# Attention and two gated MLPs on one core: another order of the first loads, and transposes without memory columns first

## The chip, the cores and the metric

One core of a Trainium2 chip runs the whole program. The metric is the device time of one execution in microseconds (us), the median over several runs; lower is better. Three runs of the kernel before took 1064.68, 1064.93 and 1065.62 us, so its median is 1064.93 us.

## The reference

The input holds q, k and v for 4 batches, 8 heads, 576 tokens and 64 numbers per head. Cut to what matters:

```python
scores = (q @ k.T) / 8, causal; a = softmax(scores); local = a @ v
q_p = phi(q)                                  # phi(x) = max(x, 0) + exp(min(x, 0))
mem_out = (q_p @ M_prev) / (q_p @ z_prev + 1e-6)
x = sigmoid(beta) * mem_out + (1 - sigmoid(beta)) * local   # 2304 tokens x 512
x = ((sigmoid(x @ w_gate) * (x @ w_val)) @ w_out)           # first MLP, 1536 wide
h = x @ w_in; out = (h * clip(h + 3, 0, 6) / 6) @ w_out2    # second MLP, 2048 wide
```

All of it is in 32-bit floats. The MLP weights come as 64-bit floats and are converted on the core.

## The kernel before, in words

The program has three phases. Phase A (`phase_a`) computes the attention and, as filler between its pieces, the first half of the first MLP; phases B and C do the rest of the MLPs. PE's order is written out by hand (the loop of lines 594 to 639 in a manual schedule). The order of DVE, ACT, POOL and SP is made by a scheduler when the program is built; each of these engines then runs its list strictly in that order.

**Visits and steps.** The attention goes by visits: two heads of one batch (a pair) and one of two ranges of query tokens. `VISITS` lists, for each batch, the four pairs with range 0 (320 tokens) and then the four with range 1 (256 tokens): visits 0 to 3, 4 to 7, 8 to 11 and so on, 32 in all. Each visit takes two steps of the loop. A step issues the scores on PE (L349, tile `s`), the row minima on DVE (L329, tile `m`; the scores are negated, so it is a minimum), and the exponentials on ACT (L367, tile `P`). Scores and the results `m` of the MLP filler share one pool of four PSUM buffers.

**Memory columns.** A row of `P` begins with 64 columns that hold phi(q) times a factor, so that one product with the stacked M_prev and v gives memory and local part together. These columns come from a chain: phi on DVE and ACT (L302 to L304), products with z_prev on POOL (L306, L310, tile `zz`), a sum and reciprocals on DVE (L311, L313, L314, and L392, L394, which also read the softmax sums `l`), and a product on POOL (L382).

**Transposes and pv.** Two or three steps after a visit's exponentials, `transpose_bank` transposes its `P` in blocks of 128x128 on PE (L413), up to four blocks in one PSUM bank, and ACT copies each bank to the tile `T` (L415). Range 0 has 11 blocks in three banks, range 1 has 18 in five. A block is named (row, column block); column block 0 holds the memory columns. One step after the last bank, `pv` (L459) multiplies `T` with the stacked M_prev and v: its first two matmuls read column block 0, the others follow by column block. For visits 0 to 7 it also spreads the factor (L429, tile `rl`) and multiplies (L470).

**Loads.** All DMAs are issued by SP. `load_visit` loads queries and keys (L262, L263, tile `qk`, two buffers), the queries by rows (L265, first part of tile `aux`), for a new batch z_prev (L270, L273, tile `zz`), and v with M_prev (L279, second part of `aux`). `gates` loads beta (L125). `w_load` loads a pair of weight blocks (L147, tile `wst`, two buffers) and `w_convert` converts it: ACT L157, DVE L158, L159, L160, L162, L163, ACT L168, DVE L169.

**The filler.** `moe_a` (L238 to L240) needs converted weights and the attention's output of a whole batch, read back by `moe_x` (tile `xs`, split on ACT L233 and DVE L234).

Of the kernel before, what the change touches and what calls it, by code (L numbers as in the profile page):

```python
# [37 lines left out]
_T = [  # L38
    [(1, 0), (2, 0), (0, 0), (3, 0), (4, 0), (1, 1), (2, 1), (3, 1), (4, 1), (2, 2), (4, 2)],
    [(2 * g + n, j) for g in range(2) for j in range(5) for n in range(2) if j <= n + 3],  # L40
]
BANKS = [[t[n : n + 4] for n in range(0, len(t), 4)] for t in _T]

UNITS = [[(0, 1), (2,)], [(3,), (4,)]]

# [35 lines left out]
class Kernel:  # L81
# [167 lines left out]
        self.visits, self.done = {}, {}  # L249

    def load_visit(self, v):
        if v >= len(VISITS):
            return
        nc = self.nc
        p, ranges = VISITS[v]
        b, h = PAIRS[p]
        qk = self.pa2.tile([128, 2, S], F32, name="qk", tag="qk")
        a = self.pa2.tile([128, 15 * D], F32, name="aux", tag="aux", bufs=3)
        rg = ranges[0]
        (t0, n), nb, j1 = RTOK[rg], len(ROWS[rg]), RANGES[rg][-1] + 1  # L260
        src = self.aux[b, h // 2]
        nc.sync.dma_start(qk[:, 0, t0 : t0 + n], self.qk[b, h // 2, :, 0, t0 : t0 + n])  # L262
        nc.sync.dma_start(qk[:, 1, : t0 + n], self.qk[b, h // 2, :, 1, : t0 + n])  # L263
        q0 = 0 if rg == 0 else 5 * D
        nc.sync.dma_start(a[:, 0 : nb * D], src[:, q0 : q0 + nb * D])  # L265
        if h == 0 and rg == 0:
            z = self.pa2.tile([128, H + H // 2, D], F32, name="zz", tag="zz", bufs=1)
            flat = lambda t: t.rearrange("p h d -> p (h d)")
            one = lambda t: t.rearrange("o h d -> o (h d)")
            nc.sync.dma_start(flat(z[:, 0:H]), one(self.zz[b : b + 1, 0:H]).broadcast_to([128, H * D]))  # L270
            for g in range(2):
                h0 = H + H // 2 * g
                nc.sync.dma_start(  # L273
                    flat(z[64 * g : 64 * g + 64, H:]),
                    one(self.zz[b : b + 1, h0 : h0 + H // 2]).broadcast_to([64, H // 2 * D]),
                )
            self.z = z
        v0 = 5 * D
        nc.sync.dma_start(a[:, v0 : v0 + j1 * 2 * D], src[:, 9 * D : 9 * D + j1 * 2 * D])  # L279
        self.visits[v] = {  # L280
            "pair": PAIRS[p],
            "ranges": ranges,
            "z": self.z,
            "qk": qk,
            "qn": a[:, 0 : nb * D].rearrange("p (r d) -> p r d", d=D),
            "v": a[:, 5 * D :].rearrange("p (j c) -> p j c", j=5),
        }
# [117 lines left out]
    def transpose_bank(self, v, rg, k):  # L405
        nc = self.nc
        pr = self.visits[v]
        if k == 0:
            pr["T", rg] = self.pa2.tile([128, 2304], F32, name="T", tag="T")
        ps = self.ps_t.tile([128, 512], F32, name="t", tag="t")  # L410
        bank = BANKS[rg][k]
        for n, (r, j) in enumerate(bank):
            nc.tensor.transpose(ps[:, 128 * n : 128 * n + 128], self.row(v, rg, r, 128 * j, 128 * j + 128), self.ident)  # L413
        c = 128 * len(bank)
        nc.scalar.copy(pr["T", rg][:, 512 * k : 512 * k + c], ps[:, :c])  # L415

    def spread(self, v, rg):

# [125 lines left out]
    def phase_a(self):  # L544
        nc, tc = self.nc, self.tc
# [10 lines left out]
        stream, c = None, 0  # L556
# [22 lines left out]
        def transposes(t, k):  # L579
            for _ in range(k):  # L580
                if tq and tq[0][0] <= t:
                    a = tq.pop(0)[1]
                    self.transpose_bank(*a)
                    if a[2] == len(BANKS[a[1]]) - 1:
                        vq.append((t + 1, a[:2]))

        t = self.step = 0
        sched = tc.manual_schedule(engines={mybir.EngineType.PE})
        sched.__enter__()
        self.load_visit(0)  # L590
        self.gates()
        self.load_visit(1)
        self.w_load()
        while t < nt or tq or vq:
            self.step = t
            fill = FILL[max(c - 1, 0)]
            first = w = 0
            if t < nt:
                v, rg, i = steps[t]
# [3 lines left out]
                first = w if w <= 512 else 320  # L603
# [19 lines left out]
            if t < nt:  # L623
                self.exponentials(v, i)
                if i == RANGES[rg][-1]:
                    self.normalize(v, rg, 5 <= t < 27)
                    if v < POST:
                        self.memory_rows(v, rg)
                    tq += [(t + (2 if v < 4 else 3), (v, rg, j)) for j in range(len(BANKS[rg]))]
            moe(fill)  # L630
# [3 lines left out]
                self.prep_phi(v + 1)  # L634
            if t >= 7 and t % 2:
                self.w_convert()
            if len(self.wstaged) < 2:
                self.w_load()
            t += 1
        while self.wstaged or self.wkeys:  # L640
# [18 lines left out]
        n = 0  # L659
# [358 lines left out]
```

## Time and profile before

| what | value |
|---|---|
| median of three runs | 1064.93 us |
| the profiled execution's own time | 1065.71 us |
| its span, first to last instruction | 1063.9 us |
| PE busy | 1038.0 us, 98% |
| DVE, ACT, POOL busy | 648.3, 538.6, 84.2 us |
| mean granted TensorE clock | 0.996 |

PE is the engine of the chain that ended last for 89% of the span. The 16,179 instructions are nearly all matmuls and weight loads of PE. The change touches the first 140 us, so the timeline of that stretch is what is to be read, engine by engine.

### The profile page before, as it was taken

What the parts mean: (1) busy time and instruction counts of PE and PEld (TensorE: products, weight loads), DVE (VectorE), ACT (ScalarE), POOL (GpSimd) and SP (SyncE); (2) the same over time, 40 slices, a digit from 0 to 9 for tenths busy, and PEclk for the clock granted to TensorE, in tenths of its full rate; (3) what the DMA queues carried; (4) which work ended last, traced back from release to release, by engine and by line L of the source; (5) the groups of instructions that cost most, each with busy time, mean ns of one, the idle gap of its engine ahead of it and who ended that gap; (6) DMA issues with size and microseconds to landing.
All of it is one profiled execution on the core that took longest, in us unless ns stands there. A gap on an engine that the chain in (4) does not pass through costs nothing.

```text
span 1063.9 us, 16179 instructions
## 1 busy us (share of the span) xinstructions
PE 1038.0 (98%) x5904; PEld 892.6 (84%) x5904; DVE 648.3 (61%) x1549; ACT 538.6 (51%) x1165; POOL 84.2 (8%) x102
## 2 busy tenths in 40 slices
PE   6799999999999999999999999999999999999998
PEld 4467678878887899999888888888888888888886
DVE  6999755454455338888888888743454433643433
ACT  6679885566556644435444344433453433633432
POOL 2213211110111000000000000410002000000000
PEclk9899999999999999999999999999999999999999
DMA  7755642424242215337686877444414542044511
GB/s 220 223 191 184 192 126 75 137 80 124 67 126 80 64 44 180 119 119 254 228 296 246 309 259 276 158 166 177 148 30 158 218 159 99 10 168 169 218 40 59
DMA packets 66239, 164.87 MB, mean 155 GB/s; under 512 B 8432, under 2 KB 41712, under 8 KB 60272
## 3 DMA queue, kind: packets, MB, share of 16 engines
q1 hardware_dynamic: 66160, 163.85, 45.2%
q8 instruction: 46, 0.75, 0.3%
q14 instruction: 33, 0.27, 0.1%
HBM read 122.76 MB, written 41.06 MB: 154 GB/s over the span
## 4 chain that ended last, share of the span: by engine, by line
PE 89%; DVE 4%; DMA 4%; ACT 1%; SPq 1%; issue 1%; POOL 0%; ACTq 0%; DVEq 0%
PE acc L866 18%; PE pa L831 9%; PE pb L831 7%; PE m L238 6%; PE g L240 6%; PE g L238 6%; PE g L239 6%; PE m L239 5%; PE m L240 5%; PE pv L459 5%; PE t L413 4%; PE s L349 4%; PE acc L238 3%; PE acc L240 3%; PE acc L239 3%; DMA xd<-xpr 1%
## 5 line engine op out<-in xcount | busy, mean ns | idle before, releaser
L866 PE MATMUL acc<-wslot,hs 128*128 128x512 f32 x864 | 227.8, 395 | 2.2 <-ACT hs L233 2.2
L866 PEld LDWEIGHTS acc<-wslot,hs 128*128 128x128 f32 x864 | 159.5, 188 | 27.7 <-ACT hs L233 3.5
L831 PE MATMUL pa<-xq,wslot 128*128 128x384 f32 x576 | 117.3, 338 | 1.1 <-ACT u L931 0.6
L831 PEld LDWEIGHTS pa<-xq,wslot 128*128 128x128 f32 x576 | 103.7, 187 | 9.9 <-ACT u L931 0.9
L240 PE MATMUL g<-xs,wslot 128*128 128x468 f32 (+1 forms) x288 | 106.4, 370 | 0.0
L239 PE MATMUL g<-xs,wslot 128*128 128x468 f32 (+1 forms) x288 | 106.3, 369 | 0.0
L238 PE MATMUL g<-xs,wslot 128*128 128x468 f32 (+1 forms) x288 | 104.1, 369 | 0.0
L367 ACT ACTIVATE P<-P,m 128x192 f32<-128x192 f32 (+4 forms) x144 | 83.9, 585 | 28.4 <-DVE m L329 27.3
L238 PE MATMUL m<-xs,wslot 128*128 128x312 f32 x288 | 94.4, 328 | 0.4 <-ACT xs L233 0.4
L239 PE MATMUL m<-xs,wslot 128*128 128x312 f32 x288 | 88.5, 307 | 0.1
L240 PE MATMUL m<-xs,wslot 128*128 128x312 f32 x288 | 88.1, 306 | 0.0
L831 PE MATMUL pb<-xq,wslot 128*128 128x384 f32 x432 | 87.8, 338 | 0.0
L831 PEld LDWEIGHTS pb<-xq,wslot 128*128 128x128 f32 x432 | 77.9, 188 | 6.3
L349 PE MATMUL s<-qk 64*128 64x320 f32 (+3 forms) x320 | 72.5, 491 | 10.3 <-DMA qk<-in_qk 7.1
L895 DVE TENSOR_TENSOR c<-pb,u 128x384 f32<-128x384 f32 x48 | 26.6, 555 | 86.7 <-ACT u L931 85.7
L843 ACT ACTIVATE r<-c,three 128x384 f32<-128x384 f32 x72 | 44.2, 614 | 63.4 <-DVE c L895 63.4
L413 PEld LDWEIGHTS t<-ident,P 128*128 128x128 f32 x464 | 53.6, 144 | 23.2 <-issue 11.9
L234 DVE TENSOR_TENSOR hs<-r,hs 128x384 fp32r<-128x384 f32 x96 | 56.5, 593 | 26.9 <-ACT hs L233 25.4
L413 PE MATMUL t<-ident,P 128*128 128x128 f32 x464 | 67.7, 284 | 3.6 <-POOL P L382 3.5
L329 DVE CUSTOM_DVE_ANT_0 P<-s,mask 128x320 f32<-128x320 f32 (+3 forms) x144 | 62.8, 451 | 13.3 <-PE s L349 13.2
L415 ACT COPY T<-t 128x512 f32<-128x512 f32 (+2 forms) x128 | 65.9, 540 | 8.4 <-PE t L413 8.3
L157 ACT ACTIVATE wf<-wst 128x512 f32<-128x512 f32 (+1 forms) x59 | 43.9, 744 | 43.4 <-DVE wst L163 36.7
(106 smaller groups left out, 1937.9 us busy)
## 6 DMA issues: line engine op xcount, KB each, us to landing
wst<-in_wm SPq DMA_DIRECT2D x68, 512.0 KB, 5.9
wslot<-wd SPq DMA_DIRECT2D x30, 1024.0 KB, 5.1
wd<-wslot SPq DMA_DIRECT2D x16, 1024.0 KB, 4.6
wslot<-wd SPq DMA_DIRECT2D x15, 768.0 KB, 6.4
wd<-wslot SPq DMA_DIRECT2D x8, 768.0 KB, 5.8
qk<-in_qk SPq DMA_DIRECT2D x32, 160.0 KB, 2.4
aux<-in_aux SPq DMA_DIRECT2D x16, 320.0 KB, 3.8
qk<-in_qk SPq DMA_DIRECT2D x16, 288.0 KB, 3.1
```

What stands on the lines that cost most here:

```text
L234: elo.tensor_tensor(lo, src, hi.bitcast(F32), op=ALU.subtract)
L238: nc.tensor.matmul(out, w[0], x[0], start=first, stop=False)
L239: nc.tensor.matmul(out, w[0], x[1], start=False, stop=False)
L240: nc.tensor.matmul(out, w[1], x[0], start=False, stop=last)
L329: self.nc.vector.tensor_tensor_reduce(out=self.row(v, rg, r, 64 + a, 64 + e), in0=ps, in1=mask, scale=-0.125, scalar=3.0e38 if a == 0 else ...
L349: nc.tensor.matmul(ps[:, : e - a], qk[rows, 0, q0 : q0 + 128], qk[rows, 1, a:e], start=True, stop=True)
L367: self.nc.scalar.activation(x, x, AF.Exp, bias=vs["m", rg][:, r : r + 1], scale=-1.0, accum_out=vs["l", rg][:, r : r + 1])
L413: nc.tensor.transpose(ps[:, 128 * n : 128 * n + 128], self.row(v, rg, r, 128 * j, 128 * j + 128), self.ident)
L415: nc.scalar.copy(pr["T", rg][:, 512 * k : 512 * k + c], ps[:, :c])
L459: nc.tensor.matmul(ps[rows, o : o + w], pr["v"][:, j, rows], T[:, c : c + w], start=(n == 0), stop=(n == last), skip_group_check=True,)
L831: nc.tensor.matmul(ps[:, :HC], w[:, i, b, cc], x[:, l, k], start=first and k == 0 and n == 0, stop=last and k == 1 and n == 2, skip_group_ ...
L866: nc.tensor.matmul(a, h[:, i, cc], w[:, l, f], start=first and f == 0 and n == 0, stop=last and f == 1 and n == 2)
```

## The change

Two things are changed.

1. `load_visit` becomes a generator, `load_parts`, which stops once after the queries and keys and the queries by rows. The program now issues these three loads for visits 0 and 1 first, then beta, then the rest (z_prev, v with M_prev) of both. The first `w_load` is no longer ahead of the loop; it comes at the end of step 2.
2. `BANKS` holds, for each bank, its place in the list of blocks. Range 0's banks are now blocks 7 to 10, 4 to 6 and 0 to 3 of the same list, in this order; range 1's are 4 to 7, 12 to 15, 16 and 17, 0 to 3, and 8 to 11. The first bank of range 0 holds no memory columns, the second one block of them and the third three. Each bank is copied to the same columns of `T` as its blocks had.

```diff
--- before.py
+++ after.py
@@ -39,7 +39,8 @@
     [(1, 0), (2, 0), (0, 0), (3, 0), (4, 0), (1, 1), (2, 1), (3, 1), (4, 1), (2, 2), (4, 2)],
     [(2 * g + n, j) for g in range(2) for j in range(5) for n in range(2) if j <= n + 3],
 ]
-BANKS = [[t[n : n + 4] for n in range(0, len(t), 4)] for t in _T]
+_B = [[(7, 11), (4, 7), (0, 4)], [(4, 8), (12, 16), (16, 18), (0, 4), (8, 12)]]
+BANKS = [[(a, t[a:e]) for a, e in b] for t, b in zip(_T, _B)]
 
 UNITS = [[(0, 1), (2,)], [(3,), (4,)]]
 
@@ -249,6 +250,10 @@
         self.visits, self.done = {}, {}
 
     def load_visit(self, v):
+        for _ in self.load_parts(v):
+            pass
+
+    def load_parts(self, v):
         if v >= len(VISITS):
             return
         nc = self.nc
@@ -263,6 +268,7 @@
         nc.sync.dma_start(qk[:, 1, : t0 + n], self.qk[b, h // 2, :, 1, : t0 + n])
         q0 = 0 if rg == 0 else 5 * D
         nc.sync.dma_start(a[:, 0 : nb * D], src[:, q0 : q0 + nb * D])
+        yield
         if h == 0 and rg == 0:
             z = self.pa2.tile([128, H + H // 2, D], F32, name="zz", tag="zz", bufs=1)
             flat = lambda t: t.rearrange("p h d -> p (h d)")
@@ -408,11 +414,11 @@
         if k == 0:
             pr["T", rg] = self.pa2.tile([128, 2304], F32, name="T", tag="T")
         ps = self.ps_t.tile([128, 512], F32, name="t", tag="t")
-        bank = BANKS[rg][k]
+        first, bank = BANKS[rg][k]
         for n, (r, j) in enumerate(bank):
             nc.tensor.transpose(ps[:, 128 * n : 128 * n + 128], self.row(v, rg, r, 128 * j, 128 * j + 128), self.ident)
         c = 128 * len(bank)
-        nc.scalar.copy(pr["T", rg][:, 512 * k : 512 * k + c], ps[:, :c])
+        nc.scalar.copy(pr["T", rg][:, 128 * first : 128 * first + c], ps[:, :c])
 
     def spread(self, v, rg):
 
@@ -587,10 +593,10 @@
         t = self.step = 0
         sched = tc.manual_schedule(engines={mybir.EngineType.PE})
         sched.__enter__()
-        self.load_visit(0)
+        loads = [self.load_parts(v) for v in range(2)]
+        next(loads[0]), next(loads[1])
         self.gates()
-        self.load_visit(1)
-        self.w_load()
+        next(loads[0], None), next(loads[1], None)
         while t < nt or tq or vq:
             self.step = t
             fill = FILL[max(c - 1, 0)]
@@ -634,7 +640,7 @@
                 self.prep_phi(v + 1)
             if t >= 7 and t % 2:
                 self.w_convert()
-            if len(self.wstaged) < 2:
+            if t >= 2 and len(self.wstaged) < 2:
                 self.w_load()
             t += 1
         while self.wstaged or self.wkeys:
```

**SP, the first loads** (qk: queries and keys; aux 128x320: queries by rows; aux 128x384: v with M_prev; wst: weights). Before, from the fourth DMA on:

```order
L270 DMA zz<-in_zz 128x512
L273 DMA zz<-in_zz 64x256 x2
L279 DMA aux<-in_aux 128x384
L125 DMA bt_sb<-in_bt 128x20
L262 DMA qk<-in_qk 128x320
L263 DMA qk<-in_qk 128x320
L265 DMA aux<-in_aux 128x320
L279 DMA aux<-in_aux 128x384
L147 DMA wst<-in_wm 128x1024 x2
```

Now, from the fourth DMA on:

```order
L267 DMA qk<-in_qk 128x320
L268 DMA qk<-in_qk 128x320
L270 DMA aux<-in_aux 128x320
L126 DMA bt_sb<-in_bt 128x20
L276 DMA zz<-in_zz 128x512
L279 DMA zz<-in_zz 64x256 x2
L285 DMA aux<-in_aux 128x384 x2
L270 DMA aux<-in_aux 128x320
L267 DMA qk<-in_qk 128x320
L268 DMA qk<-in_qk 128x320
L285 DMA aux<-in_aux 128x384
L148 DMA wst<-in_wm 128x1024 x4
```

The queries and keys of visit 1 moved ahead of zz; the weights moved behind the four loads of visit 2, and both pairs now stand together.

**ACT, the copies of visit 0's transposes** (T<-t) and the first step of the first weight conversion (wf<-wst). Before:

```order
L157 ACTIVATE wf<-wst 128x1024
L367 ACTIVATE P,l<-P,m 128x320
L415 COPY T<-t 128x512
L303 ACTIVATE phw<-phw 128x320
L415 COPY T<-t 128x512
L415 COPY T<-t 128x384
L168 CAST wslot<-wst 128x1024
```

Now:

```order
L373 ACTIVATE P,l<-P,m 128x320 x2
L421 COPY T<-t 128x512
L309 ACTIVATE phw<-phw 128x320
L421 COPY T<-t 128x384
L158 ACTIVATE wf<-wst 128x1024
L421 COPY T<-t 128x512
L373 ACTIVATE P,l<-P,m 128x192 x2
```

The weight step stood ahead of all three copies and now stands between the second and the third.

**DVE, step 11 of the loop** (P,m<-s: a row minimum; wf, wst, wslot: weight conversion). Before:

```order
L329 ISA P,m<-s,mask 128x320
L329 ISA m 128x1
L329 ISA P,m<-s,mask 128x320
L329 ISA m 128x1
L160 SCALAR_TENSOR_TENSOR wst<-wst,wf 128x1024
L311 TENSOR_REDUCE nr<-phw 128x4
L329 ISA P,m<-s,mask,m 128x256
L329 ISA m 128x1
L162 TENSOR_SCALAR wf<-wst 128x1024
L329 ISA P,m<-s,mask,m 128x256
```

Now, from the minimum of the same 320 columns on:

```order
L335 ISA P,m<-s,mask 128x320
L335 ISA m 128x1
L163 TENSOR_SCALAR wf<-wst 128x1024
L320 RECIPROCAL nr<-nr 128x4
L335 ISA P,m<-s,mask 128x320
L335 ISA m 128x1
L164 ISA wst<-wst,wf 128x1024x2
L170 TENSOR_TENSOR wslot<-wst,wslot 128x1024
L159 TENSOR_SCALAR wf<-wf 128x1024
L160 TENSOR_SCALAR wf<-wf 128x1024
L335 ISA P,m<-s,mask,m 128x256
L335 ISA m 128x1
```

Ahead of the first minimum of 256 columns five conversion steps more are done now: those of lines 163, 164, 170, 159 and 160, which are L162, L163, L169, L158 and L159 before the change. The step of line 161 (L160 before) now stands ahead of the first row shown.

## Rows read from the trace of the kernel before

**Rows 1.** Busy time by stretch (stretch, its length, each engine, granted clock, DMA share, GB/s).

```profile
0.00:19.70 19.70, 12.00 (x68) 7.41 (x69) 10.54 (x44) 10.40 (x30) 6.96 (x17) 1.00 0.79 248
19.70:64.00 44.30, 37.04 (x224) 23.82 (x226) 40.35 (x124) 33.26 (x81) 8.55 (x11) 0.92 0.62 187
...
140.00:1063.90 923.90, 916.07 (x5094) 807.02 (x5092) 531.06 (x1192) 430.28 (x892) 50.53 (x55) 1.00 0.43 148
```

**Rows 2.** Timeline, 0 to 22 us, PE (start, length, engine, line, tiles, [idle before <-releaser]).

```profile
9.40 1.14 PE L349 MATMUL s<-qk 64*128 64x192 f32 x4 [2.95 <-DMA qk<-in_qk]
...
12.54 2.55 PE L413 MATMUL t<-ident,P 128*128 128x128 f32 x11 [0.24 <-POOL P L382]
...
15.58 0.69 PE L349 MATMUL s<-qk 64*128 64x192 f32 x4 [0.48 <-DMA qk<-in_qk]
...
16.80 1.81 PE L459 MATMUL pv<-T,aux 128*64 128x320 f32 x9 [0.28 <-ACT T L415]
...
19.53 1.36 PE L349 MATMUL s<-qk 64*128 64x320 f32 x4
```

**Rows 3.** The same timeline: what waited for the first loads.

```profile
4.84 0.33 DVE L302 TENSOR_SCALAR phw<-aux 128x320 f32<-128x320 f32 x1 [3.98 <-DMA aux<-in_aux]
...
7.72 0.22 ACT L128 ACTIVATE a<-bt_sb 128x20 f32<-128x20 f32 x1 [0.33 <-DMA bt_sb<-in_bt]
...
10.47 0.33 DVE L302 TENSOR_SCALAR phw<-aux 128x320 f32<-128x320 f32 x1 [1.32 <-DMA aux<-in_aux]
...
14.62 1.12 ACT L157 ACTIVATE wf<-wst 128x1024 f32<-128x1024 f32 x1 [0.91 <-DMA wst<-in_wm]
...
15.90 0.33 DVE L302 TENSOR_SCALAR phw<-aux 128x320 f32<-128x320 f32 x1 [1.22 <-DMA aux<-in_aux]
```

**Rows 4.** The same timeline: POOL, the first product with zz, the first memory columns.

```profile
6.34 0.72 POOL L310 TENSOR_TENSOR phw<-ph,zz 128x256 f32<-128x256 f32 x1 [3.74 <-DVE ph L304]
...
11.43 1.06 POOL L382 TENSOR_TENSOR P<-ph,nr 128x320 f32<-128x320 f32 x1 [4.08 <-DVE nr L394]
```

**Rows 5.** The same timeline: ACT, last two copies of the first transposes.

```profile
17.02 0.96 ACT L415 COPY T<-t 128x512 f32<-128x512 f32 x2
```

**Rows 6.** Timeline, 20 to 75 us, PE: transposes that waited, pv that did not.

```profile
29.50 1.42 PE L413 MATMUL t<-ident,P 128*128 128x128 f32 x11 [2.35 <-POOL P L382]
...
40.72 1.51 PE L459 MATMUL pv<-T,aux 128*64 128x320 f32 x12
...
42.71 1.68 PE L349 MATMUL s<-qk 64*128 64x320 f32 x6
```

**Rows 7.** Timeline, 20 to 75 us, DVE: the steps of weight conversions.

```profile
55.47 0.69 DVE L158 TENSOR_SCALAR wf<-wf 128x1024 f32<-128x1024 f32 x1 [1.03 <-ACT wf L157]
...
57.19 0.68 DVE L159 TENSOR_SCALAR wf<-wf 128x1024 int32<-128x1024 int32 x1
...
60.54 0.69 DVE L162 TENSOR_SCALAR wf<-wst 128x1024 int32<-128x1024 uint32 x1
...
62.02 1.23 DVE L163 CUSTOM_DVE_ANT_0 wst<-wst,wf 128x2048 uint16<-128x2048 uint16 x1
...
64.77 1.22 DVE L169 TENSOR_TENSOR wslot<-wst,wslot 128x1024 fp32r<-128x1024 f32 x1
```

**Rows 8.** Timeline, 20 to 75 us, PE: a wait for xs, and scores of 448 columns.

```profile
53.97 0.41 PE L238 MATMUL m<-xs,wslot 128*128 128x312 f32 x1 [0.39 <-ACT xs L233]
...
60.08 1.61 PE L349 MATMUL s<-qk 64*128 64x448 f32 x4
```

**Rows 9.** Timeline, 84 to 140 us, PE: pv of visits 9 and 11, the latter in two rows.

```profile
109.06 1.41 PE L459 MATMUL pv<-T,aux 128*64 128x320 f32 x12
...
127.24 1.18 PE L459 MATMUL pv<-T,aux 128*64 128x320 f32 x6
...
130.03 0.86 PE L459 MATMUL pv<-T,aux 128*64 128x256 f32 x6 [1.61 <-ACT T L415]
```

**Rows 10.** Busy time by stretch, PE alone (PE busy, granted clock, DMA share, GB/s).

```profile
45.80:52.50 6.70, 5.77 (x20) 0.50 0.67 218
```

## The prediction

> **What bounds the kernel now.** I read the busy time by stretch first. From 140 us on PE is busy for 916.07 of 923.90 us [rows 1]: whatever the first 140 us lose or win on PE stays in the total, since PE's list is fixed and nothing behind it has slack to give. Between 0 and 19.7 us PE is busy for 12.00 us and DVE for 10.54, so both wait there, and the DMA share is 0.79: the first loads decide. Between 19.7 and 64 us DVE is busy for 40.35 of 44.30 us [rows 1]. That is the view that matters most: there DVE is close to full, every wait of PE hangs on its row minima or on ACT, and both run their lists strictly in order.
>
> Then I read the timelines engine by engine and followed the changed lists through them by hand: an instruction starts when its engine is free and what it reads is there, with the lengths of the rows. A sum of parts that are moved can't do this, since a part moved early on SP comes out late on ACT.
>
> **Start, the gain.** PE's first real wait is 2.95 us for the keys of visit 1 at 9.40 [rows 2]. In the new list of SP the transfers of zz, v and beta no longer stand ahead of them. These came in between 4.84 us, when the first aux ended DVE's wait, and 7.72 us, when beta ended ACT's [rows 3]: 2.9 us. The keys should land at about 6.4, PE needs them then, and the wait goes: -2.95.
>
> **Start, what takes it back.** zz now lands later, by the three loads of visit 1 (7.72 to 10.47: 2.75 us [rows 3]) and by beta (under 0.5, the rest of that stretch). POOL's first product with zz, which started at 6.34 [rows 4], starts at 9.3 to 10. The first memory columns came 5.1 us after it, at 11.43 [rows 4]; 1.32 us of that was DVE's wait for the second aux [rows 3], which falls away. So they start at 9.7 + 3.8 = 13.5 instead of 11.43, and end near 14.3 (12.8 if the chain is tighter, 14.9 if not). The transposes of visit 0 took 2.55 us for 11 [rows 2], 0.23 each. Four now run ahead of the memory columns, seven behind: they end near 15.5, against 15.09 before. The scores of visit 2 then start at about 15.5; before, at 15.58 after 0.48 us of waiting for their keys [rows 2]. Net of the start: **-0.1** (-1.5 to +0.9). Doing the blocks without memory columns first is thus what saves this place from a loss, and no more.
>
> **pv of visit 0.** On ACT the third copy of `T` now stands behind the first step of the weight conversion, and the first two matmuls of pv read exactly that copy. Before, the weights ended ACT's wait at 14.5 (the 0.91 us before 14.62), and the four loads of visit 2 came behind them, the third at 15.9 [rows 3], the fourth some 0.5 later. Now these four come first: weights at 14.5 + 1.9 = 16.4, ACT free of their step 1.0 us later, the copy (0.96 for two [rows 5]) done at 17.9. pv before started at 16.80 and the next scores at 19.53 [rows 2], its middle slowed by the same copies. Without a wait, pv and the spreading take 40.72 to 42.71 [rows 6], 2.0 us, so the next scores start at 19.9 to 20.5: **+0.8** (+0.4 to +1.5).
>
> **Transposes of visit 2.** They waited 2.35 us for POOL's columns [rows 6]. Four of eleven now go ahead, at 0.13 each: 0.5 us are certain; more only if the columns come sooner, but they hang on DVE, whose weight steps have begun. **-0.5** (-2.35 to 0). Elsewhere before 36 us I see nothing that lasts.
>
> **The first filler.** A wait of 0.39 us for the last xs [rows 8] is on ACT's cast; in the new list a weight step (1.0 us to the next start) stands ahead of that cast. **+1.0** (0 to +2).
>
> **Row minima of step 11.** This is the largest term. Ahead of the first minimum of 256 columns DVE now does five more conversion steps. Their lengths are 0.69, 1.23, 1.22, 0.69 and 0.68 us [rows 7], 4.5 together, 4.1 less the 0.08 by which each overlaps its follower. The scores of 448 columns at 60.08 [rows 8] need the PSUM buffers which these minima free, and PE stands still meanwhile. Not all is lost: DVE itself waited 1.03 us for a weight step before [rows 7], a hole that a conversion done sooner may fill. **+3.1** (+1 to +4.1). The conversions are not extra work, but what DVE saves by having done them finds PE already the bound.
>
> **pv of visits 8 to 11.** Where copies come late, pv before did six passes, 1.18 us, ahead of its 1.61 us of waiting [rows 9]; now the copy it waits for is the one that its first matmul reads, so those 1.18 us move behind the wait. At 109.06 there was no wait [rows 9]. Four such visits, at 0 to 1.2 each: **+2.4** as the middle (0 to +4.8).
>
> **Sum.** -0.1 + 0.8 - 0.5 + 1.0 + 3.1 + 2.4 = +6.7 us. The profiled execution took 1065.71 us, so 1072.4; it stands 0.8 above the median of 1064.93, so the median should be **1071.6 us**. All other moved DMAs (SP's list differs in places up to 120 us) I cost at nothing: PE shows no wait for a DMA behind 20 us other than through xs, which is priced. If that cover went, 0.5 to 1 us each.
>
> **The clock.** PE ran at a granted 0.50 (1.2 GHz) from 45.8 to 52.5 us, 5.77 us of busy time [rows 10], after a stretch with gaps; at full speed that work would take 2.9 us less. The row at 15.58 shows four score matmuls in 0.69 us where those at 9.40 took 1.14 [rows 2], so the first 13 to 15 us are slow too, though the granted clock reads 1.00. I leave both as they are in the sum. The Trainium skill (TensorE: Matmul & The Clock Gate, section on HAM oscillation) says that a wait of PE between bursts can return it to half clock, each time anew; by it the longer gap ahead of pv of visit 0 could bring a second slow stretch. The trace neither shows nor excludes this: the gap of 2.35 us at 29.50 brought none.
>
> **The rivals.**
> - *Faster: the start's gain lasts.* If zz is not what the memory columns wait for, or the weights land as early as before, PE keeps the 2.95 us, wins 0.48 and up to 2.35 at visit 2, and meets the minima no later than before: -4, 1061. For it: DVE and ACT are not full before 19.7 us [rows 1]. Against: both lists are in order, and zz and weights are behind more bytes on one queue. It decides itself by whether the first filler matmul, at 50.9 us before, comes sooner. Chance 0.10.
> - *No change.* Start and pv cancel, the five steps fall into DVE's holes (3.95 us between 19.7 and 64 [rows 1]), and the copies are in time: 0 to +2, 1065 to 1067. Chance 0.15.
> - *Slower by a second slow stretch of the clock:* another 2.9 us on top, 1074.5. Chance 0.08. The opposite, the present slow stretch gone, gives 1068.7 and is held in the forecast's range.
> - *Slower, as summed:* 1067 to 1077 by the bounds. Chance 0.67.
>
> **How the numbers follow.** A measurement of this kernel can tell about 0.2%, 2.1 us, from no change. Slower by more: 0.67 + 0.08 = 0.75; within: 0.15; faster by more: 0.10. The range leaves out most of the faster case and the far end of the bounds: 1063.5 to 1076.
>
> **What would show it.** Right: PE's wait at 9.40 gone; POOL's first product with zz near 9.7; ACT's first weight step near 16.4, and pv behind a wait on ACT of 2 us or more that ends near 18; scores of 448 columns that wait about 3 us for DVE near 60; and waits on ACT at the *start* of pv between 100 and 135 us. The first filler matmul should come within 1 us of 50.9. Wrong: if the scores of 448 columns do not wait for the minima, the largest term fails and the result is 1068.5 or less; if pv starts at 17 us, the weights were not late; if the time is below 1063, the start's gain survived the lists.

## The result, and the profile after

The changed kernel takes **1072.23 us** (median of 5 runs, 1069.61 to 1073.38) against 1065.62 us for the kernel before, run beside it: ratio 1.0059, 95% interval 1.0042 to 1.0076. That is slower by 6.6 us. The profiled execution took 1071.09 us, its span is 1069.3 us against 1063.9. Lines of the changed kernel stand 1 to 6 higher: L355 are the scores (L349 before), L335 their row minima, L419 the transposes, L421 the copies to `T`, L465 pv, L158 to L170 the weight conversion.

Busy time by stretch, kernel after (columns as in [rows 1]):

```profile
0.00:19.70 19.70, 11.96 (x49) 6.75 (x51) 10.73 (x50) 11.10 (x35) 6.39 (x18) 1.00 0.78 248
19.70:64.00 44.30, 37.05 (x223) 24.48 (x219) 43.05 (x118) 31.94 (x75) 9.29 (x9) 0.85 0.61 188
...
140.00:1069.30 929.30, 921.73 (x5128) 810.56 (x5124) 532.76 (x1203) 434.03 (x901) 52.04 (x56) 1.00 0.43 148
```

From 140 us on PE again works nearly without a hole. In the middle stretch DVE is fuller than before (43.05 us against 40.35), and the granted clock is 0.85 instead of 0.92.

Timeline, 0 to 22 us, PE, kernel after:

```profile
8.58 1.44 PE L355 MATMUL s<-qk 64*128 64x320 f32 x4
9.94 1.11 PE L419 MATMUL t<-ident,P 128*128 128x128 f32 x4
12.18 1.75 PE L419 MATMUL t<-ident,P 128*128 128x128 f32 x7 [1.12 <-POOL P L388]
13.87 1.01 PE L355 MATMUL s<-qk 64*128 64x192 f32 x4
...
18.30 2.62 PE L465 MATMUL pv<-T,aux 128*64 128x320 f32 x12 [3.01 <-ACT T L421]
```

The wait for the keys of visit 1 [rows 2] is gone, and the scores of visit 2 start at 13.87 instead of 15.58. Then pv of visit 0 stands for 3.01 us in front of its last copy, and all twelve passes follow behind it. POOL and ACT tell why. The same timeline, POOL, then ACT:

```profile
8.59 0.73 POOL L316 TENSOR_TENSOR phw<-ph,zz 128x256 f32<-128x256 f32 x1 [5.99 <-DMA zz<-in_zz]
...
11.41 0.72 POOL L388 TENSOR_TENSOR P<-ph,nr 128x320 f32<-128x320 f32 x1 [1.82 <-DVE nr L400]
```

```profile
14.03 0.56 ACT L421 COPY T<-t 128x512 f32<-128x512 f32 x1
...
15.02 0.46 ACT L421 COPY T<-t 128x384 f32<-128x384 f32 x1
16.65 1.12 ACT L158 ACTIVATE wf<-wst 128x1024 f32<-128x1024 f32 x1 [1.17 <-DMA wst<-in_wm]
17.67 0.58 ACT L421 COPY T<-t 128x512 f32<-128x512 f32 x1
```

POOL's first product with `zz` started later (8.59, released by `zz`, against 6.34 [rows 4]), but the memory columns came at 11.41 as before: the chain behind it took 2.8 us instead of 5.1. The copy that pv waits for stands behind the weight step, as forecast.

Timeline, 20 to 75 us, PE, kernel after: the next scores behind pv of visit 0 (21.91; 19.53 before [rows 2]), then the waits that answer to [rows 6] and [rows 8].

```profile
21.91 0.82 PE L355 MATMUL s<-qk 64*128 64x320 f32 x4
...
30.61 0.98 PE L419 MATMUL t<-ident,P 128*128 128x128 f32 x7 [1.91 <-POOL P L388]
...
36.00 0.81 PE L355 MATMUL s<-qk 64*128 64x320 f32 x4
...
46.08 2.71 PE L355 MATMUL s<-qk 64*128 64x256 f32 x6 [1.79 <-DVE m L335]
...
50.34 0.61 PE L239 MATMUL m<-xs,wslot 128*128 128x312 f32 x1
...
54.25 0.41 PE L239 MATMUL m<-xs,wslot 128*128 128x312 f32 x1 [1.08 <-ACT xs L234]
...
55.44 0.82 PE L355 MATMUL s<-qk 64*128 64x320 f32 x4
...
61.31 1.02 PE L355 MATMUL s<-qk 64*128 64x448 f32 x2
63.18 1.02 PE L355 MATMUL s<-qk 64*128 64x448 f32 x2 [0.86 <-DVE m L335]
```

At 36.00 PE is where it was before (36.09 then), at 55.44 it is 0.5 us behind (54.98 then). The scores of 448 columns wait 0.86 us, not 3.

Timeline, 84 to 140 us, PE: the last scores ahead of pv of visit 8, pv of visits 8 to 11, and the filler behind it. First the kernel before, what [rows 9] doesn't show:

```profile
99.88 0.81 PE L349 MATMUL s<-qk 64*128 64x320 f32 x4
100.62 2.01 PE L459 MATMUL pv<-T,aux 128*64 128x320 f32 x12
...
117.11 1.98 PE L459 MATMUL pv<-T,aux 128*64 128x320 f32 x12
...
130.83 0.41 PE L238 MATMUL m<-ha,wslot 128*128 128x312 f32 x1
```

Kernel after:

```profile
101.35 0.81 PE L355 MATMUL s<-qk 64*128 64x320 f32 x4
103.23 1.41 PE L465 MATMUL pv<-T,aux 128*64 128x320 f32 x12 [1.07 <-ACT T L421]
...
112.87 1.41 PE L465 MATMUL pv<-T,aux 128*64 128x320 f32 x12 [1.70 <-ACT T L421]
...
122.18 1.41 PE L465 MATMUL pv<-T,aux 128*64 128x320 f32 x12 [1.22 <-ACT T L421]
...
133.28 1.41 PE L465 MATMUL pv<-T,aux 128*64 128x320 f32 x12 [2.19 <-ACT T L421]
134.61 0.63 PE L239 MATMUL m<-ha,wslot 128*128 128x312 f32 x1
```

Every one now waits ahead of its first matmul, 6.2 us in all. Before there was one listed wait of 1.61 us, in the middle of pv of visit 11, and the rows of visits 8 and 10 were longer (2.01 and 1.98 us against 1.41), so pv stood a little there too. From the scores of the first row to the filler of the last PE took 30.95 us before and 33.26 after: 2.3 us more. ACT's list shows what the last copy stands behind. The same timeline, ACT, at visit 9:

```profile
109.28 0.47 ACT L421 COPY T<-t 128x384 f32<-128x384 f32 x1
109.64 1.94 ACT L407 ACTIVATE P<-P,l 128x64 f32<-128x64 f32 x5
...
112.25 0.56 ACT L421 COPY T<-t 128x512 f32<-128x512 f32 x1
```

The third copy comes 3 us behind the second, after five normalizing steps of the next visit (1.94 us) and two exponentials. In the kernel before that block also stood there, at 109.22, but behind the last copy (108.15) in this visit; where it stood ahead of it, six passes of pv were already done.

**Where the 5.4 us of span are.** I read how far PE is behind the kernel before at the same matmuls. A good mark is the scores of 320 columns right ahead of pv of visit 8: they start at 99.88 before and at 101.35 after. So the first 100 us lost 1.5 us, and what follows lost 3.9 (span less the mark, called the rest: 964.0 before, 968.0 after): 2.3 us up to the filler behind pv of visit 11, and 1.6 behind that, where PE falls to half clock (last section). The experiments below are read with the same two numbers.

### The profile page after: what moved, and what is told of

Its sections match the earlier page's. It is cut to its first block, busy times and chain, and to the rows that moved or that the text cites. A ratio compares the mean times of both kernels' runs of the same rounds, so it can differ in the third digit from the quotient of the medians.

```text
span 1069.3 us, 16177 instructions
## 1 busy us (share of the span) xinstructions
PE 1040.4 (97%) x5904; PEld 894.6 (84%) x5904; DVE 647.7 (61%) x1549; ACT 539.5 (50%) x1165; POOL 83.2 (8%) x102
## 4 chain that ended last, share of the span: by engine, by line
PE 86%; DVE 8%; ACT 3%; DMA 1%; issue 1%; SPq 0%; DVEq 0%; ACTq 0%
PE acc L872 18%; PE pa L837 9%; PE pb L837 7%; PE g L241 6%; PE m L239 6%; PE g L239 6%; PE g L240 6%; PE m L240 5%; PE m L241 5%; PE pv L465 4%; PE t L419 4%; PE s L355 3%; PE acc L239 3%; PE acc L241 3%; PE acc L240 3%; DVE P L335 1%
## 5 line engine op out<-in xcount | busy, mean ns | idle before, releaser
L355 PE MATMUL s<-qk 64*128 64x320 f32 (+3 forms) x320 | 71.3, 505 | 6.6 <-DMA qk<-in_qk 3.6
L419 PEld LDWEIGHTS t<-ident,P 128*128 128x128 f32 x464 | 54.3, 146 | 24.7 <-issue 14.3
L335 DVE CUSTOM_DVE_ANT_0 P<-s,mask 128x320 f32<-128x320 f32 (+3 forms) x144 | 62.6, 452 | 19.0 <-PE s L355 18.9
L419 PE MATMUL t<-ident,P 128*128 128x128 f32 x464 | 69.8, 287 | 3.6 <-POOL P L388 3.5
L421 ACT COPY T<-t 128x512 f32<-128x512 f32 (+2 forms) x128 | 66.2, 538 | 13.2 <-PE t L419 13.2
L465 PE MATMUL pv<-T,aux 128*64 128x256 f32 (+2 forms) x512 | 59.6, 377 | 9.8 <-ACT T L421 9.7
```

The lines of the kernel that those rows point to most:

```text
L335: self.nc.vector.tensor_tensor_reduce(out=self.row(v, rg, r, 64 + a, 64 + e), in0=ps, in1=mask, scale=-0.125, scalar=3.0e38 if a == 0 else ...
L355: nc.tensor.matmul(ps[:, : e - a], qk[rows, 0, q0 : q0 + 128], qk[rows, 1, a:e], start=True, stop=True)
L421: nc.scalar.copy(pr["T", rg][:, 128 * first : 128 * first + c], ps[:, :c])
L465: nc.tensor.matmul(ps[rows, o : o + w], pr["v"][:, j, rows], T[:, c : c + w], start=(n == 0), stop=(n == last), skip_group_check=True,)
```

## Experiments

**Theory A:** pv's first matmuls need the bank that is copied last; the loss of the banks is PE standing in front of that copy. **Rival B:** the loads are the loss (zz and weights late), as most of my sum had it. **Rival C:** the stretches at half clock come and go by themselves. The summary follows, with "mark" and "rest" from the profiled execution of each kernel. That is one execution, up to 2.9 us from the median of its kernel (first weights early: 1073.48 us against 1076.34), so a difference of 1 or 2 us in them is weak. Line numbers shift between the kernels; the tiles name the instruction.

| kernel | median us | ratio to before (95%) | mark | rest |
|---|---|---|---|---|
| before | 1065.5 | | 99.88 | 964.0 |
| changed | 1072.23 | 1.0059 (1.0042 to 1.0076) | 101.35 | 968.0 |
| banks only | 1074.57 | 1.0088 (1.0075 to 1.0101) | 107.44 | 967.3 |
| loads only | 1062.07 | 0.9972 (0.9961 to 0.9983) | 96.85 | 963.6 |
| changed, old banks from visit 8 | 1066.75 | 1.0013 (1.0005 to 1.0022) | 102.35 | 964.0 |
| changed, old banks in visits 0 to 3 | 1069.92 | 1.0037 (1.0024 to 1.0050) | 98.13 | 970.0 |
| changed, first weights early | 1076.34 | 1.0102 (1.0087 to 1.0117) | 105.92 | 965.8 |
| changed, pv multiplies memory columns last | 1073.60 | 1.0074 (1.0058 to 1.0090) | 106.48 | 965.7 |
| loads only, the same order of pv | 1072.16 | 1.0061 (1.0046 to 1.0075) | 101.65 | 967.7 |
| before, first weights late | 1072.45 | 1.0067 (1.0049 to 1.0085) | 103.58 | 965.8 |
| before, keys of visit 1 early | 1070.97 | 1.0059 (1.0042 to 1.0076) | 102.43 | 965.9 |
| before, conversion cut | 1068.98 | 1.0032 (1.0020 to 1.0044) | 106.10 | 961.1 |
| keys early, conversion cut | 1064.08 | 0.9984 (0.9976 to 0.9993) | 101.97 | 961.6 |
| changed, conversion cut | 1069.51 | 1.0030 (1.0020 to 1.0041) | 101.96 | 965.7 |

**Banks only.** The loads of before, the new banks:

```diff
+        self.load_visit(0)
+        self.gates()
+        self.load_visit(1)
+        self.w_load()
...
-            if t >= 2 and len(self.wstaged) < 2:
+            if len(self.wstaged) < 2:
```

> The changed banks of transposes alone, with the loads in the order of before. Theory A (pv's first matmuls wait for the bank that is copied last, in visits 8 to 11): in the changed kernel these waits, with what the clock loses behind them, carry the lag from 1.5 us at 101 to 6 us at 150, so most of that should stay here: 1068.5 to 1071.5, with four waits of 1 us or more on ACT at the start of pv between 100 and 140 us. Rival B (the loads: zz and weights land late, and the delay is handed down): the banks alone cost nothing, 1064 to 1066.5. Rival C (stretches at half clock that come and go): the time follows the number of such stretches and not the waits.

Measured 1074.57 us: the banks alone lose 9.1 us, more than the whole change. Rival B's 1064 to 1066.5 falls. PE's waits between 100 and 140 us, this kernel (waiting, what for: us in total, times, longest):

```profile
PE pv L465 <- ACT T L421: 5.5, 4, 2.2
```

Four waits, as theory A wants, though one is 0.41 us only; but only 3.3 us of the loss stand behind the mark, and 7.6 ahead of it, which A had not put there (this execution took 1076.44 us, 1.9 above the median).

**Loads only.** The changed kernel with the banks of before:

```diff
-_B = [[(7, 11), (4, 7), (0, 4)], [(4, 8), (12, 16), (16, 18), (0, 4), (8, 12)]]
+_B = [[(0, 4), (4, 8), (8, 11)], [(0, 4), (4, 8), (8, 12), (12, 16), (16, 18)]]
```

> The new order of loads alone, with the banks of before. Theory A: only the lag of the first 100 us is left, 1.5 us, and the transposes behind the memory columns cost up to 1 us more at the start: 1066 to 1069, with no wait at the start of pv between 100 and 140 us. Rival B: nearly all the loss is here, 1070.5 to 1073. Rival C: as the number of stretches at half clock says.

Measured 1062.07 us: **faster than both kernels**, by 3.4 us against before and 10.2 against the changed one. My range for it began at 1066. Timeline, 0 to 22 us, PE, this kernel:

```profile
11.82 2.61 PE L419 MATMUL t<-ident,P 128*128 128x128 f32 x11 [1.86 <-POOL P L388]
14.36 1.01 PE L355 MATMUL s<-qk 64*128 64x192 f32 x4
...
15.59 1.18 PE L465 MATMUL pv<-T,aux 128*64 128x320 f32 x6
17.52 0.65 PE L465 MATMUL pv<-T,aux 128*64 128x256 f32 x4 [0.74 <-ACT T L421]
...
18.87 0.81 PE L355 MATMUL s<-qk 64*128 64x320 f32 x4
```

The transposes now wait 1.86 us for the memory columns, which is what the new banks were to avoid, and the scores of visit 2 come 0.5 us later than in the changed kernel (13.87). But pv of visit 0 does half its passes ahead of the last copy, and the next scores start at 18.87, against 21.91 in the changed kernel and 19.53 before [rows 2]. The first filler matmul comes at 47.49, 3.4 us sooner than before (50.93).

**Old banks from visit 8 on.**

`BANKS_O` is built like `BANKS`, from the old `_B`:

```diff
-        first, bank = BANKS[rg][k]
+        first, bank = (BANKS if v < 8 else BANKS_O)[rg][k]
```

> The changed kernel, but visits from 8 on use the banks of before. Theory A: the waits at the start of pv between 100 and 140 us go, and with them about 4 us: 1067 to 1069. The granted clock between 130 and 140 us should read 1.00 again, since PE doesn't stand still ahead of it. Rival B: no change against the changed kernel, 1071 to 1073. Rival C: 1071 to 1073 also, with the clock still low between 130 and 140 us.

Measured 1066.75 us, 5.5 less than the changed kernel, slightly better than A had it. The rest behind the mark is that of before, 964.0. PE's waits between 100 and 140 us:

```profile
PE pv L466 <- ACT T L422: 2.2, 2, 1.2
```

Both are of the kind that the kernel before shows, inside pv with two or six passes done, and no stretch at half clock is left between 100 and 160 us. Of the 4.0 us that the rest wins, 1.8 come by the filler behind pv of visit 11 (31.43 us from the mark, against 33.26 in the changed kernel); the others come behind it, where the changed kernel has that stretch.

**First weights early.** The changed kernel, `w_load` ahead of the loop again and the condition on `t` taken out:

```diff
         next(loads[0], None), next(loads[1], None)
+        self.w_load()
...
-            if t >= 2 and len(self.wstaged) < 2:
+            if len(self.wstaged) < 2:
```

> The changed kernel, but the first weights are loaded ahead of the loop again, behind the loads of visits 0 and 1. Theory A: pv of visit 0 no longer waits 3 us for its last copy, and PE is 1 to 2.4 us earlier near 22 us; the waits of visits 8 to 11 stay, so 1069.5 to 1072. Rival B: the late weights are the loss, 1065 to 1067.5. Rival C: as the number of stretches at half clock says.

Measured 1076.34 us, worse than A and B had it, and 4.1 us above the changed kernel. PE waits 2.63 us for the keys of visit 2 at 16.25, now behind the weights; pv of visit 0 still waits, and the next scores come at 22.32. So in the changed kernel the late weights are no loss but a gain.

**pv with the memory columns last.** The banks and copies stay; in visits 0 to 3 and 8 to 11 pv begins with block columns 1 and 2. Block column 0 is split, since its 64 columns that nothing else writes need a start of their own:

```diff
+            for g in range(2):
+                o, f = 64 * g, 256 * (1 - g)
+                ops[g] = [
+                    (1, o, 640 + 256 * g, 256, True, False),
+                    (2, o + 128, 1152 + 128 * g, 128, False, False),
+                    (0, o, 320 * g + o, 256, False, True),
+                    (0, f, 320 * g + f, 64, True, True),
+                ]
```

> The changed kernel, but pv of visits 0 to 3 and 8 to 11 multiplies the memory columns last: it begins with what the banks copied first hold, and four of its matmuls can run ahead of the copy of the last bank. Transposes, copies and loads stay as in the changed kernel. Theory A (the loss is pv standing in front of the last bank): the loss of the banks, 10 us over the loads alone at 1062.1, goes for the most part: 1062 to 1066. Rival D (the new order of transposes and copies itself is dearer, whichever part pv reads first): 1070 to 1073, as the changed kernel.

Measured 1073.60 us: a miss for A as a whole, and half a hit. The rest falls from 968.0 to 965.7, the waits at pv from 6.2 to 3.8 us between 100 and 145. But the mark is 5.1 us later than in the changed kernel. Timeline, 0 to 45 us, PE, this kernel:

```profile
15.49 1.55 PE L475 MATMUL pv<-T,aux 128*64 128x256 f32 x8 [0.24 <-ACT T L421]
18.01 1.33 PE L475 MATMUL pv<-T,aux 128*64 128x256 f32 x8 [0.97 <-ACT T L421]
...
20.34 1.44 PE L355 MATMUL s<-qk 64*128 64x320 f32 x4
...
31.39 1.75 PE L419 MATMUL t<-ident,P 128*128 128x128 f32 x7 [3.25 <-POOL P L388]
33.07 1.87 PE L355 MATMUL s<-qk 64*128 64x448 f32 x4
```

pv of visit 0 gains as wanted, the next scores start 1.6 us sooner (20.34 against 21.91). Then the transposes of visit 2 wait 3.25 us for POOL instead of 1.91, and the scores behind them run in 1.87 us for four instead of 1.22, at a granted clock of 0.50 between 32 and 36 us.

**The same order of pv with the old banks and the new loads.** The diff of the run above, with the old `_B` as in the loads only. pv's second matmul now reads the bank that is copied last:

```diff
-_B = [[(7, 11), (4, 7), (0, 4)], ...
+_B = [[(0, 4), (4, 8), (8, 11)], ...
+                ops[g] = [
+                    (1, o, 640 + 256 * g, 256, True, False),
...
```

> The loads alone (1062.1), with the banks of before, but with the order of pv of the run above in visits 0 to 3 and 8 to 11: its second matmul now reads the bank that is copied last. Theory A: pv waits again although transposes and copies stand as in the faster kernel, and loses 4 to 10 us: 1066 to 1072, with waits on ACT at the start of pv between 95 and 135 us. Rival D: 1061 to 1064.

Measured 1072.16 us against 1062.07: 10 us lost by the order of pv alone, with banks and loads those of the fastest kernel. PE's waits between 100 and 140 us:

```profile
PE pv L475 <- ACT T L421: 3.7, 3, 2.2
```

4.8 us of the loss are ahead of the mark and 4.1 behind it, 1.6 of these by the filler behind pv of visit 11 (33.19 us from the mark against 31.61). So which part pv reads first does cost time with transposes and copies as they were, and rival D falls as the whole of the loss. But theory A isn't shown as the whole either: with this order of pv the new banks take 1073.60 us and the old ones 1072.16, so it gave back nothing of what the new banks cost. Ahead of the mark the two changes even add up (96.85 with neither, 101.35 with the banks, 101.65 with the order of pv, 106.48 with both), which A doesn't explain.

**The halves of the loads.** First only the weights late, then only the keys early:

```diff
         self.load_visit(1)
-        self.w_load()
...
-            if len(self.wstaged) < 2:
+            if t >= 2 and len(self.wstaged) < 2:
```

> The kernel before, with the first weights late (from the end of step 2) as the one change. With the new banks, late weights were worth 4.1 us (1072.2 against 1076.3). Theory E (they are the gain of the loads, since visit 2's loads no longer queue behind 2 x 512 KB of weights, and DVE's and ACT's first conversion steps stand later): 1061 to 1063.5. Rival F (the early keys of visit 1 are the gain): 1065 to 1066.5. My prediction's step (late weights cost 0.8 at pv of visit 0 and more at the first filler): 1066 to 1070.

> The kernel before, with only the first half of the change in the loads: queries and keys of visit 1 early, zz later, the weights ahead of the loop as before, the banks as before. Theory E: no gain, 1065 to 1067.5, as the wait for the keys comes back at visit 2, whose loads then stand behind the weights. Rival F: 1061 to 1063.5.

Measured 1072.45 and 1070.97 us: **each half alone loses (7 and 5.5 us), both together gain 3.4.** Theories E and F both fall, and so does my prediction's step (1066 to 1070 for the weights late); a reading that adds one part's gain to the other's can't hold here. Timeline, 20 to 75 us, PE, weights late only:

```profile
40.83 1.22 PE L349 MATMUL s<-qk 64*128 64x256 f32 x2 [3.15 <-DVE xpr L470]
...
57.78 0.63 PE L238 MATMUL m<-xs,wslot 128*128 128x312 f32 x1 [3.68 <-ACT xs L233]
```

Scores wait for a PSUM buffer that DVE's product L470 frees, and the filler for an `xs`, each a wait that the kernel before has at 1.0 and 0.39 us at most. With the keys early only, the waits are 2.58 us for POOL at 29.32 and 1.45 us for DVE at 41.25. One pattern is common to these two, the banks only and the changed kernel with its weights early: the fourth weight conversion starts on ACT between 43.6 and 49.2 us. In the kernel before, the changed one and the loads only it starts between 52.1 and 54.3. That is no cause shown: the two kernels with the other order of pv are as slow and have it at 53.2 and 57.0. PE also ran at half clock for longer, some 17 us with the weights late and 10 with the keys early, against 7 in the kernel before (added up from the granted clock by half microseconds).

**Old banks in visits 0 to 3.** The counterpart of the run with old banks from visit 8 on:

```diff
-        first, bank = BANKS[rg][k]
+        first, bank = (BANKS if v >= 4 else BANKS_O)[rg][k]
```

> The changed kernel, but visits 0 to 3 use the banks of before, the others the new ones (the counterpart of the run with the old banks from visit 8 on). If the two places of the banks' loss are separate, this one gives back the other part: 10.2 us is the whole (1072.2 against 1062.1 for the loads alone), 5.5 of it was from visit 8 on, so 4.7 comes back here: 1066.5 to 1068.5, with the waits on ACT at the start of pv between 100 and 140 us still there. If the early part is only handed down to the later one, more comes back: 1063 to 1065.5. If the early part is not the banks: 1070 to 1073.

Measured 1069.92 us: 2.3 us come back, half of what I had. At the mark it is 3.2 us (98.13 against 101.35), but the waits behind it grow to 6.9 us. The two places of the loss are real, and they aren't quite separate.

**Conversion cut.** Five of DVE's six steps of a conversion and one of ACT's two are left out in the first part:

```diff
-        for hif in self.value(st):
+        hif = st[:, :, :, 1].bitcast(F32)
+        for hif in self.value(st) if self.wide == 1 else [hif]:
             nc.scalar.copy(sl[:, 0], hif)
```

> The kernel before without five of DVE's six steps and the first of ACT's two steps of each weight conversion in the first part of the program (the weights there then are not the right ones); loads, casts and all work of PE stay. DVE loses about 30 us of its busy time before 140 us. Theory G (between 20 and 66 us PE waits for lists of DVE and ACT in which conversion steps stand ahead of what it needs): 1055 to 1062. Otherwise 1064 to 1066. It is the base for the next two.

> The early keys alone (1071.0, 5.5 us above the kernel before), without the same conversion steps. Theory G: the loss is the place of conversion steps in DVE's and ACT's lists, so it goes: within 2 us of the kernel before without these steps. Rival H (the late zz and the loads of visit 2 behind the weights cost it by themselves): 3.5 to 6 us above that kernel.

> The changed kernel without the same conversion steps. Theory A with G: pv's waits for its last bank stay in part, as the copies stand in ACT's list behind exponentials too: 2 to 6 us above the kernel before without these steps. If the conversions were all of the loss of 6.6 us: within 1 us of it.

Measured 1068.98, 1064.08 and 1069.51 us. The first is the surprise: 38.6 us less work on DVE ahead of 140 us, and the kernel is **3.4 us slower**. Theory G, as I had put it, falls. DMA issues between 30 and 62 us (tensor, queue, number, KB each, median us from issue to landing), the kernel with the conversion cut, then the kernel before:

```profile
wst<-in_wm SPq DMA_DIRECT2D x9, 512.0 KB, 5.7
```

```profile
wst<-in_wm SPq DMA_DIRECT2D x4, 512.0 KB, 4.4
```

Timeline, 36 to 64 us, the kernel with the conversion cut, DVE, then PE:

```profile
41.96 0.29 DVE L303 TENSOR_SCALAR phw<-aux 128x256 f32<-128x256 f32 x1 [2.12 <-DMA aux<-in_aux]
```

```profile
44.10 2.66 PE L350 MATMUL s<-qk 64*128 64x448 f32 x4 [3.04 <-DVE m L330]
```

A conversion that is done sooner frees its staging buffer sooner, so nine weight loads fall into this stretch instead of four. DVE stands 2.12 us for queries by rows. Their load was issued at 36.82, behind two of weights at 35.43, and took 5.1 us; the same load of the kernel before, issued at 36.45, took 2.1. The row minima stand behind it in DVE's list, and PE waits 3.04 us for them. PE's longest wait, 4.49 us for `xs` at 60.89, is not a slow read: that read of `xc` took 2.2 us, but it was issued only at 58.19. PE also ran at half clock for some 20 us of this execution, against 7 in the kernel before. So the trace shows one place where loads that come sooner hold up what PE needs next; how much of the loss that is isn't shown. The keys early are now a gain of 4.9 us over their base where they had been a loss of 5.5, outside what either G or H wanted: the same change of loads wins or loses with what else stands in the lists. The changed kernel is 0.5 us above its base, as if the conversions were all of the loss, but by two parts of opposite sign: its mark is 4.1 us earlier, its rest 4.6 longer. Behind the mark the old banks give 961.1 and 961.6 and the new ones 965.7, so there they seem to cost without the conversions too; but the loads of the two with old banks differ from those of the changed kernel, and only that one has a stretch at half clock there (near 133 us).

## Why the prediction was right, and where it was not

The direction, the size (1071.6 forecast, 1072.2 measured) and the range were right. The sum came out right in part by luck. Its terms were read from a trace, and from trace to trace the loss is 5.4 us, not 6.7; the medians are 6.6 apart since the changed kernel's profiled execution lies 1.1 us below its median. And errors cancel. Two sums were wrong in themselves: seven transposes of 0.23 us behind 14.3 end at 15.9 and not at 15.5, and the bounds of the terms add up to 1062.5 and 1078.2, not to 1067 and 1077. Term by term, on the changed kernel's trace:

- **Start, forecast -0.1.** Measured -1.7 at the scores of visit 2. The step that failed is that zz holds back the memory columns, which I had at 13.5: the first product with zz was 2.3 us later, the columns were not (11.41 against 11.43), since it started at 8.59 and not at 9.7, and the chain behind it took 2.8 us and not the 3.8 that I had left it.
- **pv of visit 0, forecast +0.8.** The weight step came at 16.65 (forecast 16.4) and pv's wait ended at 18.30 (forecast 17.9), but the next scores are at 21.91, not at 19.9 to 20.5: from -1.7 to +2.4, 4.1 us. I had taken pv and the spreading at the 2.0 us that they need at 40.72 [rows 6]. Here they took 3.6, pv alone 2.62 for 12 passes against 1.51 there. And I blamed the weights; with the same weight step ahead of its last copy, the loads alone have the next scores at 18.87. It is the bank, which pv's first matmul reads. Of the 3.0 us between 21.91 and 18.87, 1.8 are pv and the spreading at the slow rate of the start (2.62 and 1.28 us, against 1.41 and 0.72 for visit 1); pv of the loads alone runs at the later rate here (1.18 us for six passes, as in [rows 9]). Why the slow rate lasted longer in the changed kernel is not shown.
- **Transposes of visit 2, forecast -0.5,** and nothing else up to 36 us. Measured: all of the lag came back by 36.00, also because PE before waited 0.96 and 0.68 us for copies ahead of pv of visit 2 and inside it (32.82 and 34.75), and the changed kernel didn't. So up to here the forecast's +0.2 met -0.1.
- **First filler, forecast +1.0.** It came 0.6 us sooner (50.34 against 50.93), and the waits for xs are 1.4 against 0.4 us; +0.5 at 55.44.
- **Row minima of step 11, forecast +3.1, the largest term.** The five steps do stand ahead of the minima, and the lag grows from 0.5 to 2.5 us by the transposes behind the scores of 448 columns (64.13 against 61.62). But by 81 us it is 1.2: the kernel before paid a wait of 0.96 us at 73.40 that the changed one doesn't. The term measured some +0.8. The list is what held PE: DVE worked without a hole from 54.2 to 63.5. 1.8 of the 2.0 us of growth were there already at 59.62 (57.37 before), in a stretch at half clock; had PE been at full speed, it would have had to wait for the minima that much longer, by this reading. I had seen that a conversion done sooner could fill a hole of DVE, and had counted only the hole in DVE, not PE's next wait.
- **pv of visits 8 to 11, forecast +2.4.** Measured +3.9 behind the mark (968.0 less 964.0, unrounded). Four pairs with the same loads agree: banks new against old 968.0 to 964.0 (changed, and old banks from visit 8), 967.3 to 964.0 (banks only, and before), 970.0 to 963.6 (old banks in visits 0 to 3, and loads only), and by the order of pv alone 967.7 to 963.6. One speaks against it: with keys and weights early, 965.8 with the new banks and 965.9 with the old, where a wait of 1.82 us comes after two passes of pv. The mechanism was right, and so was the size of what it names: 2.3 us by the filler behind pv of visit 11. The other 1.6 come behind it, with the stretch at half clock that the term left out (below).

Together: -0.1 up to 36 us, +0.6 to 55, +0.8 to 81, +0.2 to the mark and +3.9 behind it make the 5.4 us of the profiles. By my own sign of being wrong, a failed largest term should have meant 1068.5 or less. It came to a quarter of its forecast; 1.5 us more behind the mark and the 1.2 us between the profiles and the medians made up for it.

As parts of the change: I had the loads as a loss and the banks as a small one. The runs show the reverse for the loads. Without the banks they gain 3.4 us, and the rival to which I gave 0.10 ("the start's gain lasts", 1061, the first filler sooner) is what the loads alone do (1062.07, filler at 47.49). The banks take 10.2 us from that.

**What stays open:** why either half of the loads loses alone. The profiles show which waits grow, that conversions move earlier in the lists and that PE is at half clock for longer. Open too is why the banks cost some 4.5 us ahead of the mark (101.35 against 96.85), of which 3.0 are there behind pv of visit 0 (21.91 against 18.87). Cutting the conversions did not isolate their place, since it moved the weight loads too, and holding ACT's and DVE's lists fixed under another order of loads wasn't tried.

## What to carry to other kernels

Before reordering producers, look which of them the consumer's *first* instruction reads: its last-finished part belongs behind as much of the consumer's work as possible, or the whole consumer queues behind it. Measure the parts of a change singly and together: here two losses were a gain together. And work taken off an engine that isn't the bound is not free time: it released transfers sooner here, and one of these stood ahead of a load for which DVE, and then PE, waited.

## What the runs showed of the hardware

The clock had a larger part than I gave it. Busy time by stretch, PE alone, kernel after (PE busy, granted clock, DMA share, GB/s):

```profile
32.00:36.00 4.00, 4.00 (x29) 0.57 0.92 330
45.80:52.50 6.70, 6.42 (x23) 0.51 0.76 254
56.00:60.00 4.00, 4.00 (x20) 0.57 0.29 116
134.50:141.50 7.00, 7.00 (x25) 0.51 0.61 174
```

The kernel before had the second of these alone [rows 10]; its clock is 1.00 in the other three. The last begins right behind the longest late wait of pv (2.19 us at 133.28), and PE falls back by 2.3 us from there on, from 3.8 us behind at 134.61 to 6.1 at 148.93, although it is busy throughout. In all PE was at half clock for some 20 us of the changed kernel's profile and 7 of that before. This was my rival of a second slow stretch, with a chance of 0.08. A stretch near 138 us appears in the changed kernel, in the banks alone and with the first weights early, which all have a wait of 2.2 us there, and not in the kernel before, the loads alone or with old banks from visit 8 on. So in these profiles it comes only with a wait. But not each wait brings one: behind 2.06 us at 136.84 (memory columns last in pv) and 2.19 us at 133.50 (the same order of pv with the old banks) the granted clock stays at 1.00. With old banks in visits 0 to 3 the wait of 2.23 us at 120.47 brought one, those of 2.58 and 2.12 us none. The Trainium skill (TensorE: Matmul & The Clock Gate, section on HAM oscillation) says that waits between bursts can return PE to half clock; the trace agrees at 134.5 to 141.5 us, at 0.51, and not behind the waits that brought none.

Rival C, that such stretches come and go by themselves, holds in part: the mean granted clock of whole executions is 0.990 to 0.998 in 48 of the kernel before and 0.990 to 0.997 in five of the changed one. But it is not the main loss. At 0.997 nine executions of the kernel before took 1063.82 to 1065.80 us and one of the changed kernel 1069.61, so at an equal clock at least 3.8 of the 6.6 us are left. And four kernels with 10 us at half clock in their profiles (loads only, old banks from visit 8, the order of pv with the old banks, keys early) have spans from 1060.4 to 1069.3 us.

In the first 20 us of the changed kernel the granted clock reads 1.00, and yet equal work takes nearly twice as long: pv of visit 0 took 2.62 us for 12 passes, pv of visit 1, at 25.41, 1.41. Lengths of rows from the very start are thus no measure for the same instruction later, nor the other way round.
